# Moving the end of one norm and joining two small products in a fused attention and feed-forward kernel

## The chip, the core and the metric

The kernel runs on one core of a Trainium2 chip. The metric is the device time of one execution in microseconds (us). The core has five engines with a queue each: TensorE (PE) multiplies matrices, VectorE (DVE) and ScalarE (ACT) work elementwise, GpSimd (POOL) copies a little here, and SyncE (SP) issues most DMAs. An instruction starts when the ones ahead of it in its engine's queue have started and the semaphores that it waits for have been raised.

## The reference

An attention without softmax, normalised, is followed by a multiplicative feed-forward block, all in fp32. The batch is 8, with 8 heads, 576 tokens and 64 columns per head; the feed-forward block has 4608 tokens of width 512 and an inner width of 1024.

```python
kv = np.einsum('bhsd,bhse->bhde', k, v)
out = np.einsum('bhsd,bhde->bhse', q, kv)
rms = np.sqrt(np.mean(out * out, axis=-1, keepdims=True) + 1e-06)
attn = out / rms * g_norm
x = attn.transpose(0, 2, 1, 3).reshape(B * S, H * D)
a = x @ w1
b = x @ w2
h = a * b @ w3
result = h @ w_out
```

## The kernel before

**Algebra.** w3 and w_out are multiplied ahead of the loop into one matrix (w3o), and g_norm is multiplied into w1 and w2. The two matrix products that remain, the gates (x times w1 and w2) and the projection (a·b times w3o), are made in Strassen-Winograd form: seven products of half-sized blocks in place of eight, with sums and differences made on DVE, and, for part of the panels of the later groups and their projection, in two levels of it.

**Groups.** The 576 tokens of a batch are 512 and 64 left over. A group `T` is the 512 tokens of batch `T`; the leftovers of all eight batches make one more group. The order is `groups = [0, ..., 6, 8, 7]`, so the seventh group is `T = 6`. While the feed-forward block of group `T` runs, the attention of batch `b = T + 1` is made in pieces between its products. The pieces are lists `fs[0..7]` and `ends[0..7]` in `steps(b)`; `between()` runs one piece at fixed places. In the first group (`T = 0`, batch 1) the pieces come two in each of the panels p = 1, 2, 3 and two in the projection; `fs[2]` and `fs[3]` are the two pieces of panel 2. In the later groups two come in the one-level panel 2, four in the two-level panels (`gates_of_two`: after the third and sixth of the seven products of each of two halves of the weights), two in panel 3. There `fs[3]` follows the sixth product of the first half, and `fs[4]` the third product of the second half.

**Attention of a batch.** `begin_kv(g)` is the k-v product of four heads (L335). `product(h)` is the q-kv product of half the heads (64 matmuls of 64x64 in the trace, L413), into two PSUM banks; `product_left()` is the same for the 64 leftovers of two batches (32 matmuls, L432), made with every odd batch. Each is followed by `norm`: for each of the two banks a square on ACT (L380) and a reduce on DVE (L381); after them one square root on ACT (L385), a reciprocal (L387) and two multiplications on DVE (L390) that write `xn` or `xn_left`. `norm` is a generator with two stops, after the reduces and after the square root, so that its parts can be given different places. For batches above 2 both squares write one buffer, `sq0`, else two. The normalised `xn` is turned by a DMA: copies that split the words (L294 on ACT or POOL), a DMA transpose on SP (L298), and copies that join them (L308). q is turned in the same way (L296, L298, L308).

**Winograd panel.** `winograd` makes the seven products of a panel (L724) in PSUM banks r1, r2, r3. The copies of sums that are used again leave PSUM on ACT (L742) under the names p1, p5, u2 and u3; u3 is the sum in r1 ahead of the last product, which goes on in r1 and so waits for u3's copy. p1's copy, in these panels to `inner_sums`, frees r1 for the third product of the panel. `done` adds and multiplies on DVE (L897, L898, L894). With `copy_first` (panel 3 of the later groups) the first sum is copied from bank to bank (L751). The two-level products are L1016; their sums leave PSUM by `copy_seven` on ACT (L1065, L1066) and `add_seven` on DVE (L1069, L1070), and are finished on DVE (L1078 to L1102).

**PSUM.** There are two pools of banks, `mm` with five and `at` with three. The next bank of a pool is the one used longest ago, and its first matmul waits until the last reader is done.

**Order.** The orders of PE, POOL and SP are the program's own (`manual_schedule`). ACT and DVE, outside some stretches, are ordered at build time by a list scheduler; `tc.issue_after(x)` gives what follows a place behind the instruction `x` in that order. `slots` holds calls to be made right after a named copy, as in

```python
slots.setdefault(("p1", "p1"), []).insert(0, (all_of, rest))
```

which ends a norm behind the copy p1 in panel 1. In the first group `a.finish(0)` or `begin_first` makes the first q-kv product of the next batch; for batch 1 it is `a.finish(0)`, the whole norm at once, in the first piece of panel 2.

Of the kernel before, what the change touches and what calls it, by code (L numbers as in the profile page):

```python
# [22 lines left out]
def kernel(  # L23
# [36 lines left out]
    B, H, S, D = q.shape  # L60
# [4 lines left out]
    FIRST_OF_TWO = 2  # L65
# [12 lines left out]
    ps_at = ctx.enter_context(tc.tile_pool(name="ps_at", bufs=3, space=PSUM))  # L78
# [5 lines left out]
    def bank(pool, tag):  # L84
        return pool.tile([P, 512], FP32, name=tag, tag=tag)

    loaded, copies, adds = {}, {}, {}
# [26 lines left out]
    NF = KF // 2  # L114
# [139 lines left out]
    def all_of(steps):  # L254
        for _ in steps:
            pass
# [61 lines left out]
    def attention(b):  # L318
# [80 lines left out]
        def product(h):  # L399

            of_mm = b and (h == 0 or b <= FIRST_OF_TWO or b % 2 == 0)
            o_ps = [bank(*((ps_mm, "mm") if of_mm else (ps_at, "at"))), bank(ps_at, "at")]
            for m in range(4):
                r, e = 2 * h + m // 2, m % 2
                for i in range(2):
                    n = 2 * m + i
                    for t in range(2):
                        tokens = slice(t * L, (t + 1) * L)  # L410
                        for l in range(2):
                            rows = slice(l * D, (l + 1) * D)
                            nc.tensor.matmul(  # L413
                                o_ps[l][tokens, n * D:(n + 1) * D],
                                lhsT=qT[r][rows, e, i, tokens],
                                rhs=kv_b[rows, m // 2 ^ l, e, h, :],
                                start=True,
                                stop=True,
                            )
            xn = st[h] = work.tile([P, 2, 2, 4, D], FP32, name="xn", bufs=1)  # L420
            return norm(o_ps, [xn[:, :, l].rearrange("p i m d -> p m i d") for l in range(2)])
# [82 lines left out]
        def finish(h):  # L504
            all_of(product(h))
# [8 lines left out]
    def batch(b):  # L514
        if b not in batches:
            batches[b] = attention(b)
        return batches[b]

    slots, stage = {}, [None]

    def run_slot(key, behind):
        for f, *args in slots.pop(key, []):
            with tc.issue_after(behind.ins):
                f(*args)
# [51 lines left out]
    def steps(b):  # L576

        a = batch(b)
        a.start()
        more = b + 1 < B
        fs, ends = ([[] for _ in range(8)] for _ in range(2))

        def turn(i, f, *args, next_group=False):

            t = []

            def begin():  # L590
                t.append(f(*args))
                next(t[0])
                next(t[0])

            fs[i].append((begin,))
            (to_end if next_group else ends[i + 1]).append((lambda: all_of(t[0]),))

        if to_end:

            ends[0] += [(lambda: nc.gpsimd.tensor_copy(tick, late["p5"][:, 0, 0:1]),), *to_end]  # L600
        to_end.clear()
        odd = b % 2
        by_scalar, in_two = b >= FIRST_OF_TWO, b > FIRST_OF_TWO
        if b == 1:
            early.extend(a.q_two_by_dma(r) for r in (0, 1))
            q_first = list(early)
            fs[0].append((a.begin_kv, 0))

            def end_first():
                for t in q_first:  # L610
                    with tc.issue_after(copies["u3"][-1].ins):
                        next(t)
                    all_of(t)

            ends[1].append((end_first,))
        def begin_first():
            rest = a.product(0)
            next(rest)
            slots.setdefault(("p1", "p1"), []).insert(0, (all_of, rest))

        fs[2 if b == 1 else 1] += [
            (a.begin_kv, 1), (begin_first,) if by_scalar and not in_two else (a.finish, 0),
        ]
        if b == 1:
            last = {}

            def begin(name, behind, f, *args):
                last[name] = f(*args)
                with tc.issue_after(copies[behind][-1].ins):
                    next(last[name])  # L630
                next(last[name])

            def end(name, behind):
                with tc.issue_after(copies[behind][-1].ins):
                    next(last[name], None)
                all_of(last[name])

            fs[2].append((begin, "q2", "u2", a.q_two_by_dma, 2))
            fs[3].append((begin, "q3", "u3", a.q_two_by_dma, 3))
            fs[3].append((begin, "left", "u3", a.q_left_by_dma))  # L640
            fs[4].append((begin, "x", "u3", a.x_by_dma, 0, nc.scalar.copy))
            ends[4] += [(end, "q2", "p1"), (end, "q3", "p5")]
            ends[5] += [(end, "x", "u2"), (end, "left", "u3")]
        elif by_scalar:
            turns_by_scalar(b)
        else:
            turn(1, a.q_two_by_dma, 2, 3)
            turn(2, a.x_by_dma, 0)
            if odd:
                turn(1, a.q_left_by_dma)  # L650
        second = 5 if b == 1 else 4
        if more:
            if not (in_two and odd):
                fs[second].append((batch(b + 1).begin_kv, 0))
        fs[second].append((a.finish, 1))
        if odd:
            fs[3 if in_two else second + 1].append((a.product_left,))
        if b == 1:
            turn(6, a.x_by_dma, 1)
            turn(7, a.x_left_by_dma, next_group=True)  # L660
        else:
            if not by_scalar:
                turn(5, a.x_by_dma, 1)
            if odd:
                turn(5, a.x_left_by_dma, next_group=more)
        if more and not by_scalar:
            turn(7 if b == 1 else 5, batch(b + 1).q_two_by_dma, 0, 1, next_group=True)
        if more:
            fs[7 if odd else 0].append((load_q_left, b + 1))
        return iter([lambda s=e + f: [f(*args) for f, *args in s] for e, f in zip(ends, fs)])  # L670
# [211 lines left out]
    def gates(T, p, between, ready=lambda name: None):  # L882
        def done(name, one, two):
            multiply(name, one, two)
            ready(name)

        def multiply(name, one, two):

            dst = ab[int(name[1]) - 1][:, p, int(name[2]) - 1, :]
            if two is None:  # L890
                c = late_pool.tile([P, N], FP32, name="c21")
                copied = nc.scalar.copy(c, one[:, 0, :])
                run_slot((stage[0], name), copied)
                adds.setdefault(name, []).append(nc.vector.tensor_mul(dst, c, one[:, 1, :]))  # L894
                return
            c = late_pool.tile([P, 2, N], FP32, name="c")
            adds.setdefault(name, []).append(nc.vector.tensor_add(c, one, two))  # L897
            nc.vector.tensor_mul(dst, c[:, 0, :], c[:, 1, :])  # L898

        winograd(  # L900
            lambda name, w, c: wa[p][name][:, w, c, :],
            lambda name, c: xb[T][name][:, c, :],
            NP // 2, done, between, T == 0 or p + 1 < NF,
            places=(2, 1, 0) if T not in IN_TWO else (0, 1, 2) if p + 1 == NF else (2, 0, 1),
            copy_first=T in IN_TWO and p + 1 == NF,
            first=bank(ps_at, "at") if T in IN_TWO and p + 1 == NF and T % 2 and T + 2 < B else None,
        )


# [471 lines left out]
    IN_TWO = (*range(FIRST_OF_TWO, B - 1), *TWICE)  # L1381
# [9 lines left out]
    with tc.manual_schedule(  # L1391
# [44 lines left out]
        first = batch(0)  # L1436
# [52 lines left out]
    for n, T in enumerate(groups):  # L1489
# [29 lines left out]
        if T in IN_TWO:  # L1519
            p = 2  # L1520
            stage[0] = "p2"
            with tc.issue_after(adds["out"].ins):
                sum_x(T)
            gates(T, p, between)
            if T in TWICE:
                in_order = tc.manual_schedule(engines={mybir.EngineType.DVE})
                in_order.__enter__()
            gates_of_two(T, between)
            of_two = sum_ab_two()
            for _ in range(3):  # L1530
                of_two.pop(0)()
        else:
            of_two = []
        for p in range(NF):
# [3 lines left out]
            if T and p + 1 == NF:  # L1538
# [15 lines left out]
                gates(T, p, between, lambda name: all_of(f() for f in following[name]))  # L1554
                continue
            gates(T, p, between if T or p else lambda: None)
            if T == 0:

# [92 lines left out]
```

## Time and profile before

| | us |
|---|---|
| median of three runs | 744.86 |
| lowest and highest | 744.60, 745.33 |
| the profiled execution's own time | 745.0 |
| its span on the core | 743.1 |
| PE busy | 736.6 |
| DVE busy | 629.4 |
| ACT busy | 378.7 |

The profile is of one execution. Its own time is 1.9 us above its span; that part lies outside the recorded instructions. The granted clock of TensorE was 1.00 throughout. A row of a timeline gives the start, the duration from the first start to the last end, engine, line, operation, the output and input tiles by name, shapes, and the number of instructions; in brackets is the idle time of the engine ahead of it, and what ended that. Starts of neighbouring rows on one engine may be closer than the durations, since instructions overlap at their ends: the distance of two starts is what an instruction takes of its engine's time. The first group's panels start at 83.2 us and its last panel at 123.6 us; the seventh group runs from 531 to 603 us.

### The profile page before, as it was taken

What the parts mean: (1) busy time and instruction counts of PE and PEld (TensorE: products, weight loads), DVE (VectorE), ACT (ScalarE), POOL (GpSimd) and SP (SyncE); (2) the same over time, 40 slices, a digit from 0 to 9 for tenths busy, and PEclk for the clock granted to TensorE, in tenths of its full rate; (3) what the DMA queues carried; (4) which work ended last, traced back from release to release, by engine and by line L of the source; (5) the groups of instructions that cost most, each with busy time, mean ns of one, the idle gap of its engine ahead of it and who ended that gap; (6) DMA issues with size and microseconds to landing.
All of it is one profiled execution on the core that took longest, in us unless ns stands there. A gap on an engine that the chain in (4) does not pass through costs nothing.

```text
span 743.1 us, 16816 instructions
## 1 busy us (share of the span) xinstructions
PE 736.6 (99%) x6843; PEld 659.5 (89%) x6843; DVE 629.4 (85%) x1233; ACT 378.7 (51%) x652; POOL 21.8 (3%) x29
## 2 busy tenths in 40 slices
PE   8999999999999999999999999999999999999998
PEld 6455788888899999999999999999999999999997
DVE  6987998967869689978996899689969987997797
ACT  6687778424552575257526752576277313212321
POOL 0000000132000000010000001000001000000000
PEclk9999999999999999999999999999999999999999
DMA  9996934599999698869886988588848662565454
GB/s 307 366 321 208 263 108 122 122 331 307 281 307 321 176 264 271 267 159 284 258 265 158 304 255 263 184 279 241 278 101 220 220 212 87 176 215 162 135 198 135
DMA packets 135456, 169.65 MB, mean 228 GB/s; under 512 B 78036, under 2 KB 110804, under 8 KB 135380
## 3 DMA queue, kind: packets, MB, share of 16 engines
q1 hardware_dynamic: 132928, 154.16, 69.6%
q10 hardware_dynamic: 2452, 14.42, 5.7%
q8 instruction: 54, 0.88, 0.5%
q14 instruction: 22, 0.18, 0.1%
HBM read 130.55 MB, written 20.71 MB: 204 GB/s over the span
## 4 chain that ended last, share of the span: by engine, by line
PE 96%; DVE 1%; ACT 1%; DMA 1%; issue 0%; SPq 0%; ACTq 0%
PE mm L724 37%; PE mm L1274 23%; PE mm L1016 21%; PE mm L694 7%; PE at L335 2%; PE at L724 2%; PE at L413 1%; PE mm L413 1%; PE at L681 1%; DMA raw<-in_moe_w_out_dram 1%; PE at L1317 0%; DVE ab L162 0%; PE at L432 0%; ACT w_sb L133 0%; DVE chunks L169 0%
## 5 line engine op out<-in xcount | busy, mean ns | idle before, releaser
L1065 ACT COPY slots<-mm 128x512 f32<-128x512 f32 x88 | 51.7, 587 | 125.7 <-PE mm L1274 83.1
L724 PE MATMUL mm<-xT,w_sb 128*128 128x256 f32 x448 | 102.9, 379 | 0.0
L724 PEld LDWEIGHTS mm<-xT,w_sb 128*128 128x128 f32 x448 | 84.4, 190 | 11.5 <-issue 0.5
L724 PE MATMUL mm<-xc,ws 128*128 128x256 f32 x336 | 76.1, 379 | 0.0
L724 PEld LDWEIGHTS mm<-xc,ws 128*128 128x128 f32 x336 | 63.8, 190 | 8.7
L742 ACT COPY slots<-mm 128x512 f32<-128x512 f32 x59 | 34.6, 587 | 70.9 <-PE mm L724 65.5
L694 PE MATMUL mm<-chunks,ab 128*128 128x512 f32 x128 | 60.7, 605 | 0.7 <-DVE chunks L172 0.7
L1069 DVE TENSOR_TENSOR slots<-mm,slots 128x512 f32<-128x512 f32 x66 | 45.1, 683 | 17.3 <-PE mm L1016 17.3
L1066 ACT COPY slots<-mm 128x384 f32<-128x384 f32 x88 | 42.4, 482 | 25.8 <-PE mm L1274 23.1
L1016 PE MATMUL mm<-ws,w3o_sb 128*128 128x128 f32 x350 | 53.9, 275 | 0.0
L381 DVE TENSOR_REDUCE inv<-sq 128x8 f32<-128x512 f32 (+1 forms) x40 | 24.6, 629 | 29.9 <-ACT sq L380 29.9
L1274 PE MATMUL mm<-w3o_sb,ab 128*128 128x128 f32 x368 | 49.0, 276 | 0.0
L1016 PEld LDWEIGHTS mm<-ws,w3o_sb 128*128 128x128 f32 x350 | 46.4, 192 | 0.0
L1274 PEld LDWEIGHTS mm<-w3o_sb,ab 128*128 128x128 f32 x368 | 45.4, 192 | 0.6
L1274 PE MATMUL mm<-w3o_sb,raw 128*128 128x128 f32 x340 | 43.5, 275 | 0.0
L694 PEld LDWEIGHTS mm<-chunks,ab 128*128 128x128 f32 x128 | 21.6, 190 | 22.4 <-issue 14.4
L1274 PEld LDWEIGHTS mm<-w3o_sb,raw 128*128 128x128 f32 x340 | 40.7, 192 | 0.0
L724 PE MATMUL mm<-xc,w_sb 128*128 128x256 f32 x160 | 38.6, 384 | 0.3 <-ACT slots L742 0.3
L724 PE MATMUL mm<-xT,ws 128*128 128x256 f32 x160 | 38.1, 381 | 0.0
L1070 DVE TENSOR_TENSOR slots<-mm,slots 128x384 f32<-128x384 f32 x66 | 36.4, 551 | 1.9 <-PE mm L1274 1.9
L308 ACT COPY xT<-xn 128x1024 uint16<-128x1024 uint16 x28 | 32.5, 1168 | 3.3 <-DMA xn<-xT 3.3
L724 PEld LDWEIGHTS mm<-xc,w_sb 128*128 128x128 f32 x160 | 29.7, 190 | 4.9 <-ACT slots L742 0.7
(243 smaller groups left out, 1650.8 us busy)
## 6 DMA issues: line engine op xcount, KB each, us to landing
w3o_sb<-w_l SPq DMA_DIRECT2D x21, 896.0 KB, 4.9
w3o_sb<-w3o_l SPq DMA_DIRECT2D x18, 896.0 KB, 6.8
raw<-in_moe_w_dram SPq DMA_DIRECT2D x31, 512.0 KB, 7.4
raw<-w3o_l SPq DMA_DIRECT2D x15, 896.0 KB, 4.9
w3o_sb<-w3o_l ACTq DMA_DIRECT2D x14, 896.0 KB, 4.6
k_sb<-in_k_dram SPq DMA_DIRECT2D x16, 576.0 KB, 5.1
v_sb<-in_v_dram SPq DMA_DIRECT2D x16, 576.0 KB, 6.3
q_sb<-in_q_dram SPq DMA_DIRECT2D x32, 256.0 KB, 4.3
```

The lines of the kernel that those rows point to most:

```text
L308: copy(words(dst), src)
L335: nc.tensor.matmul(ps[r * D:(r + 1) * D, :], lhsT=k_sb[rows, r, cols], rhs=v_sb[rows, r, cols], start=(j == 0), stop=(j == JS - 1),)
L381: adds["norm"] = nc.vector.tensor_reduce(out=inv[:, i], in_=sq.rearrange("p (h d) -> p h d", d=D), axis=AX.X, op=ALU.add)
L694: nc.tensor.matmul(sums_ps[half][m], lhsT=w3T[half, c][:, m, :], rhs=chunks[:, c, 1, :], start=(c == 0), stop=(c == KF - 1),)
L724: nc.tensor.matmul(ps[:, u, :], lhsT=lhsT(a_name, u, c), rhs=rhs(b_name, c),  start=(u == 0 and c == 0 and new), stop=(c == chunks - 1), s ...
L742: copies.setdefault(name, []).append(nc.scalar.copy(t, ps))
L1016: nc.tensor.matmul(ps[place // 4][:, place % 4, :], lhsT=x, rhs=y, start=new and place // 4 not in seen, stop=True, skip_group_check=True,)
L1065: nc.scalar.copy(z[:, 0:4], ps[0])
L1066: return nc.scalar.copy(z[:, 4:7], ps[1][:, 0:3])
L1069: nc.vector.tensor_add(z[:, 0:4], ps[0], z[:, 0:4])
L1070: nc.vector.tensor_add(z[:, 4:7], ps[1][:, 0:3], z[:, 4:7])
L1274: nc.tensor.matmul(ps[place // 4][:, place % 4, :], lhsT=x[:, c, :], rhs=y[:, c, :], start=new and place // 4 not in seen, stop=(c == 1), ...
```

## The change

In the first group, the end of the first norm of batch 1 (the square root, the reciprocal, the multiplications) is no longer made in one go with its beginning. `begin_first` makes the product, the squares and the reduces; a new function `end_first_norm` in the next piece gives the square root and what follows a place behind u3's copy of panel 2. For the other batches `begin_first` does what it did.

In the seventh group, `product_left` of batch 7 moves from `fs[3]` to the front of `fs[4]`, so that its matmuls come right ahead of those of the second q-kv product, with no product of the feed-forward block between them. The first bank of that q-kv product becomes a `mm` bank in place of an `at` bank, and the first bank of panel 3 an `at` bank in place of a `mm` bank. The DMAs and copies that turn the leftovers stay in their pieces.

```diff
-            of_mm = b and (h == 0 or b <= FIRST_OF_TWO or b % 2 == 0)
+            of_mm = b and (h == 0 or b <= FIRST_OF_TWO or b % 2 == 0 or b == B - 1)
...
+        rest_of_norm = []
+
         def begin_first():
-            rest = a.product(0)
-            next(rest)
-            slots.setdefault(("p1", "p1"), []).insert(0, (all_of, rest))
+            rest_of_norm.append(a.product(0))
+            next(rest_of_norm[0])
+            if b > 1:
+                slots.setdefault(("p1", "p1"), []).insert(0, (all_of, rest_of_norm[0]))
+
+        def end_first_norm():
+            with tc.issue_after(copies["u3"][-1].ins):
+                next(rest_of_norm[0])
+            all_of(rest_of_norm[0])
 
         fs[2 if b == 1 else 1] += [
-            (a.begin_kv, 1), (begin_first,) if by_scalar and not in_two else (a.finish, 0),
+            (a.begin_kv, 1), (a.finish, 0) if in_two else (begin_first,),
         ]
+        if b == 1:
+            fs[3].append((end_first_norm,))
...
         if odd:
-            fs[3 if in_two else second + 1].append((a.product_left,))
+            at = 4 if b == B - 1 else 3 if in_two else second + 1
+            fs[at].insert(0, (a.product_left,))
...
-            first=bank(ps_at, "at") if T in IN_TWO and p + 1 == NF and T % 2 and T + 2 < B else None,
+            first=bank(ps_at, "at") if T in (*range(FIRST_OF_TWO + 1, B - 2, 2), B - 2) and p + 1 == NF else None,
```

## The prediction

> **What bounds the kernel now.** I read the page first, then the waits of TensorE (PE), then a table of windows over the panels of the first group, then the timelines of PE, ScalarE (ACT) and VectorE (DVE) around the two places that the diff touches, and last the order in which the built program issues its instructions on each engine, before and after the change. That order is fixed at build time, so the steps below can be worked out on it with durations from the trace. The page:
>
> ```profile
> PE 736.6 (99%) x6843; PEld 659.5 (89%) x6843; DVE 629.4 (85%) x1233; ACT 378.7 (51%) x652; POOL 21.8 (3%) x29
> ```
>
> PE is the bound in every stage, so a microsecond that PE waits is a microsecond of the span, and one that DVE or ACT works longer is nothing until PE waits for it. In PE's list of waits one line lies behind the start-up:
>
> ```profile
> PE mm L724 <- ACT slots L742: 0.3, 1, 0.3
> ```
>
> That is the wait which the first edit is aimed at. Its price is seen better in the windows of two panels of the first group with the same PE work (28 Winograd matmuls, one k-v product, one q-kv product):
>
> ```profile
> 108.62:123.61 14.99, 14.70 (x194) 12.55 (x193) 12.35 (x25) 11.71 (x22) 0.00 (x0) 1.00 0.45 129
> 123.61:138.03 14.42, 14.42 (x193) 12.63 (x192) 14.42 (x38) 9.58 (x13) 0.00 (x0) 1.00 0.68 135
> ```
>
> The columns are the window, its length, then busy time and count of PE, PEld, DVE, ACT, POOL, and the granted clock. The panel with the wait is 14.99 − 14.42 = 0.57 us longer, at a clock of 1.00 in both. So at most 0.57 us are to be had here.
>
> **First edit: the end of the norm behind u3's copy.** PE's timeline, ACT's and DVE's:
>
> ```profile
> 117.87 3.62 PE L724 MATMUL mm<-xT,w_sb 128*128 128x256 f32 x16
> 121.78 1.99 PE L724 MATMUL mm<-xc,w_sb 128*128 128x256 f32 x8 [0.29 <-ACT slots L742]
> 123.61 1.89 PE L724 MATMUL mm<-xT,w_sb 128*128 128x256 f32 x8
> 125.33 3.62 PE L724 MATMUL mm<-xc,ws 128*128 128x256 f32 x16
> ```
>
> ```profile
> 119.49 0.59 ACT L380 ACTIVATE sq<-at 128x512 f32<-128x512 f32 x1
> 120.94 0.31 ACT L385 ACTIVATE inv<-inv,eps_col 128x16 f32<-128x16 f32 x1 [0.86 <-DVE inv L381]
> 121.16 0.56 ACT L742 COPY slots<-mm 128x512 f32<-128x512 f32 x1
> 123.52 1.99 ACT L294 COPY xT<-xn 128x1024 uint16<-128x1024 uint16 x2
> 126.02 0.59 ACT L742 COPY inner_sums<-mm 128x512 f32<-128x512 f32 x1 [0.24 <-DVE c L897]
> ```
>
> ```profile
> 119.63 1.28 DVE L381 TENSOR_REDUCE inv<-sq 128x8 f32<-128x512 f32 x2 [2.64 <-ACT sq L380]
> 122.48 0.68 DVE L390 TENSOR_TENSOR xn<-at,inv 128x512 f32<-128x512 f32 x1
> ```
>
> The copy of u3 (121.16) stood behind the square root (120.94), which waited 0.86 us for the reduces; the last product of the panel waited for that copy. In the new order the copy stands right behind the second square: 119.97 to 120.6, before PE wants it at 121.3. The wait goes and the last panel starts at 123.61 − 0.57 = 123.04. What is late next is the same norm. On DVE the new order puts between the reduces and the second multiplication of xn (L390) three of the four sums of the next weights, and two adds ahead of it. By the starts of neighbouring rows a 128x512 operation takes 0.60 us, a 128x256 one 0.335, the reciprocal 0.16. After the reduces (120.83): five 128x512 (the add of c12, two sums ws, the sum w_sb, the add of c22) and one 128x256 between them, then the reciprocal, another 128x256, the first multiplication and the add of c11, in all 7 × 0.60 + 2 × 0.335 + 0.16 = 5.03 us. So the second multiplication starts at 125.86 and ends at 126.54, against 123.16 now: 3.4 us later.
>
> Two ACT copies xT<-xn (L294) read that xn, 0.95 us each by their starts, and the built order leaves them where they were against the next panel: ahead of its first copy, inner_sums<-mm. So that copy, queued behind a waiting instruction, now starts at 126.57 + 2 × 0.95 = 128.46 and ends at 129.05. It frees the bank into which PE's third product of the panel accumulates. That product started at 125.33 + 1.73 = 127.06 before, would be due at 126.49 after, and now waits to about 129.07: a new wait of 2.6 us where one of 0.57 went. Net 129.07 − 127.06 = 2.0, and 0.1 for the restart (the old wait cost 0.46 us of start and 0.57 of panel): **+2.1 us**. Bounds: 1.9 if the restart costs nothing, 2.4 if the next copies (two transposes' copies of 1.06 us stand between them) also come 0.2 to 0.3 us late; by the rows they come 0.2 us early. The fourth sum ws, now behind the norm, is done by 127.8 and wanted at 130.8; SP and POOL keep their order.
>
> [...] The rows show a clock of 1.00 around the present wait of 0.3 us, and no row has a wait as long as the new one.
>
> **Second edit: the leftovers' product joined to the second q-kv product.** PE's rows around the leftovers' block of the seventh group:
>
> ```profile
> 554.48 0.39 PE L1016 MATMUL mm<-sq,raw 128*128 128x128 f32 x2
> 554.79 0.69 PE L432 MATMUL at<-kv_sb,qT_left 64*64 64x64 f32 x32
> 555.42 0.71 PE L1016 MATMUL mm<-xc,w_sb 128*128 128x128 f32 x4
> 555.97 0.39 PE L1016 MATMUL mm<-ws,w_sb 128*128 128x128 f32 x2
> ```
>
> Two L1016 rows take 0.223, so the block holds PE from 554.71 to 555.97 − 0.447 = 555.52: 0.81 us. Its 32 small matmuls at 0.0145 each (64 of L413 take 0.93) are 0.46; the other 0.35 is the change to 64x64 and back, which a joined block pays once. PE gains **0.35 us**, if nothing makes it wait.
>
> Now the norms of both products come in one stretch. For these batches all squares share one buffer (sq0), so each square waits for the reduce of the one before: four handovers ACT to DVE, two of which now stand ahead of copies that PE needs. I work in the clock of before (the first edit shifts all by 2.1). The joined block starts at 561.87 − 0.81 = 561.06; after it the products of weights 3, 4, 5, 6 start at 562.71, 564.27, 565.84 and 567.40, the panel at 568.96. The DVE sums of product 1 (3.4 us from L1069 to L1084) start at 559.5 (PE goes on from that product at 560.21 − 0.81), without the old leftovers' norm ahead, and free DVE at 562.9. Then: reduce of the first leftovers' square to 563.3, second square to 563.7, reduce to 564.15, square root to 564.5, reciprocal and two multiplications to 565.4, while ACT squares the first half of the q-kv product by 565.0; its reduce 565.4 to 566.1, second square 566.14 to 566.73, and only then the second copy of product 3 (L1066):
>
> ```profile
> 565.05 0.60 ACT L380 ACTIVATE sq<-at 128x512 f32<-128x512 f32 x1 [0.31 <-DVE inv L381]
> 565.54 0.47 ACT L1066 COPY slots<-mm 128x384 f32<-128x384 f32 x1
> 568.38 1.29 DVE L390 TENSOR_TENSOR xn<-at,inv 128x512 f32<-128x512 f32 x2 [0.25 <-ACT xT L308]
> 575.39 0.59 ACT L742 COPY slots<-mm 128x512 f32<-128x512 f32 x1
> ```
>
> That copy ends at 567.1 instead of 566.0. Product 5 wants its bank at 565.84 + 0.89 = 566.73: **wait 0.4**. The add (L1069) behind the second reduce ends at 568.04; product 6 wants its bank at 567.80: **wait 0.25**. The two copies L308 behind L1066 end at 569.44, so xn (568.38 above) starts at 569.47, 1.09 late; DVE works without a pause from there, so the u2 copy (575.39) moves to 576.48 and ends at 577.07, while PE, by then 0.3 late, wants it at 576.53: **wait 0.55**. Sum: −0.35 + 0.4 + 0.25 + 0.55 = +0.85, and DVE's rest lag of 0.2 shows at most 0.1 in the projection: **+0.9 us**. Bounds: −0.35 if all three waits stay hidden, +1.5 if each is 0.2 longer than worked out.
>
> At nothing: the q-kv product's first half in a mm bank and the panel's first product in an at bank. Groups three and five have it so, and their L413 blocks and L724 products take what these take. The at bank is free from 565.5, 3.4 us ahead of its use; if it were not, PE would wait for the difference. The leftovers' multiplication ends 4.5 us later, so POOL's copy (1.04 us) and SP's transpose move with it, and the w3o load queued behind that transpose is issued at 567.9 instead of 566.15; it lands about 4.9 us later, at 572.8, and is wanted at 581.4. The copies to x_left end near 573, wanted at 591.2.
>
> **Sum.** +2.1 + 0.9 = +3.0 us: span 743.1 to 746.1, the profiled execution's own 745.0 to 748.0; against the median of the runs shown, 744.86, it is 747.9.
>
> **Rivals.** (1) Only the second edit behaves as its words say: the waits at 566.7, 567.8 and 576.5 do not come, because the handovers from ACT to DVE and back leave more room than my rows give. Then +2.1 − 0.35 = 1.75: 746.6. Against it: three separate places must hold. (2) Faster: xn is ready early enough for the two L294 copies to be out of the way. It decides at one point: the second multiplication must end by 126.49 − 0.59 − 1.90 = 124.0 us. Then both gains are net: −0.57 − 0.35 = −0.92, and with the second edit's waits hidden 743.9. For it, today's row ends at 123.16; against it, the new order has 5.0 us of DVE work ahead and DVE is busy without a pause there. (3) As rival 2 in the first group, but the second edit's waits come: −0.57 + 0.9 = +0.3: 745.2, no change. (4) The lag spreads: the next copies of the first group's last panel come late too, and each wait of the second edit is longer: +2.4 + 1.5 = 3.9: 748.8.
>
> **How the numbers follow.** Forecast 0.72, rival 1 0.14, rival 2 0.03, rival 3 0.03, rival 4 0.08. The range takes in forecast, rival 1 and rival 4: 746.6 to 748.9. About 0.2% (1.5 us) is what a measurement of this kernel can tell from no change; faster by that 0.03, within it 0.04, slower 0.93.
>
> **What would show it.** Right: no PE wait on u3's copy; a new PE wait of about 2.6 us in the first group's last panel, released by ACT's inner_sums copy, with L294 ahead of it starting near 126.6; three short PE waits in the seventh group; the L432 and L413 rows in one stretch. Wrong: xn done by 124, an ACT copy inner_sums ahead of L294, or no PE wait behind the joined block.

## The result and the profile after

| | before | after |
|---|---|---|
| median, us | 744.96 (744.60 to 745.33, 6 runs) | 748.48 (747.68 to 750.10, 6 runs) |
| ratio | | 1.005, 95% interval 1.0037 to 1.0063 |
| profiled execution, own time and span | 745.0, 743.1 | 750.1, 748.2 |
| mean granted clock of the profiled execution | 1.000 | 0.998 |

The change makes the kernel 3.5 us slower. The prediction was 747.9 us with a range of 746.6 to 748.9. The profiled execution of after is one of the longer ones. In the changed kernel every line number from L617 on is larger by up to 11: L724 is L735, L742 is L753, L1016 is L1027, L1066 is L1077. The whole trace of after lies 0.24 us later than that of before from the start-up on, ahead of both edits; this is taken off where starts are compared.

TensorE's waits after, behind the start-up (us in total, times, longest):

```profile
PE mm L735 <- ACT inner_sums L753: 2.4, 1, 2.4
...
PE mm L1027 <- ACT slots L1077: 0.3, 1, 0.3
PE at L735 <- ACT slots L753: 0.3, 1, 0.3
```

The wait on u3's copy is gone, and a wait of 2.4 us on the inner_sums copy has come. The last two lines are of the seventh group. The first group, on PE's, ACT's and DVE's timelines of after:

```profile
121.56 1.89 PE L735 MATMUL mm<-xc,w_sb 128*128 128x256 f32 x8
123.29 1.89 PE L735 MATMUL mm<-xT,w_sb 128*128 128x256 f32 x8
125.02 1.89 PE L735 MATMUL mm<-xc,ws 128*128 128x256 f32 x8
129.29 2.98 PE L735 MATMUL mm<-xc,ws 128*128 128x256 f32 x8 [2.38 <-ACT inner_sums L753]
132.06 2.64 PE L735 MATMUL mm<-xT,ws 128*128 128x256 f32 x8
```

```profile
120.20 0.59 ACT L753 COPY slots<-mm 128x512 f32<-128x512 f32 x1
121.17 0.31 ACT L385 ACTIVATE inv<-inv,eps_col 128x16 f32<-128x16 f32 x1 [0.38 <-DVE inv L381]
...
126.77 1.99 ACT L294 COPY xT<-xn 128x1024 uint16<-128x1024 uint16 x2 [2.85 <-DVE xn L390]
128.66 0.58 ACT L753 COPY inner_sums<-mm 128x512 f32<-128x512 f32 x1
```

```profile
126.05 0.68 DVE L390 TENSOR_TENSOR xn<-at,inv 128x512 f32<-128x512 f32 x1
```

u3's copy (120.20) stands ahead of the square root (121.17), and its product (121.56) no longer waits. The second multiplication of xn starts at 126.05, the two L294 copies wait for it, and the inner_sums copy stands behind them, at 128.66. PE's third product of the panel waits for it until 129.29.

One thing in these rows was not expected: the two products behind the wait take 2.77 and 2.48 us by their starts, and a product of this form takes 1.73 to 1.84. The windows of after over the wait and these two products (length, then busy time and count of PE, PEld, DVE, ACT, POOL, then the granted clock), and the same of a run with the first edit alone:

```profile
126.75:129.29 2.54, 0.16 (x1) 0.00 (x0) 2.54 (x8) 2.52 (x4) 0.00 (x0) 1.00 0.00 0
129.29:132.06 2.77, 2.77 (x8) 2.25 (x9) 2.77 (x10) 2.56 (x3) 0.00 (x0) 0.66 0.11 38
132.06:134.54 2.48, 2.48 (x10) 2.08 (x9) 1.30 (x4) 0.58 (x1) 0.00 (x0) 0.70 0.76 218
```

```profile
126.75:129.29 2.54, 0.15 (x1) 0.00 (x0) 2.54 (x8) 2.52 (x4) 0.00 (x0) 1.00 0.00 0
129.29:131.13 1.84, 1.83 (x9) 1.63 (x10) 1.84 (x7) 1.84 (x3) 0.00 (x0) 1.00 0.00 0
131.13:132.85 1.72, 1.72 (x9) 1.52 (x8) 1.72 (x6) 1.22 (x2) 0.00 (x0) 1.00 0.47 152
```

The idle stretch is the same in both, 2.54 us long with PE busy for the first 0.15. In after the clock then falls to half; by the trace's records of the clock for 3.41 us, from 130.16 on, 0.87 us after PE had gone on. This costs (2.77 − 1.84) + (2.48 − 1.72) = 1.69 us. In the other execution it stays at 1.00.

The seventh group, PE and ACT:

```profile
565.00 0.69 PE L432 MATMUL at<-kv_sb,qT_left 64*64 64x64 f32 x32
...
571.19 0.49 PE L1027 MATMUL mm<-ws,raw 128*128 128x128 f32 x2 [0.34 <-ACT slots L1077]
...
581.14 1.99 PE L735 MATMUL at<-xT,w_sb 128*128 128x256 f32 x8 [0.26 <-ACT slots L753]
```

```profile
567.18 0.38 ACT L380 ACTIVATE sq<-at 128x256 f32<-128x256 f32 x1 [1.05 <-DVE inv L381]
...
570.17 0.60 ACT L380 ACTIVATE sq<-at 128x512 f32<-128x512 f32 x1 [0.86 <-DVE inv L381]
570.67 0.47 ACT L1077 COPY slots<-mm 128x384 f32<-128x384 f32 x1
```

The second square of each norm waits for a reduce, and the copy L1077, which PE waits for at 571.19, stands behind the last of them.

The profiled execution adds up. Against before PE is 0.24 us late at the start, 4.02 in the second group (so first edit 2.10 and clock 1.68 between) and 5.11 in the projection of the seventh group (second edit 1.09).

### The profile page after: what moved, and what is told of

It reads as the page before. It is cut to its first block, busy times and chain, and to the rows that moved or that the text cites. A ratio compares the mean times of both kernels' runs of the same rounds, so it can differ in the third digit from the quotient of the medians.

```text
span 748.2 us, 16823 instructions
## 1 busy us (share of the span) xinstructions
PE 739.1 (99%) x6843; PEld 661.3 (88%) x6843; DVE 629.8 (84%) x1233; ACT 378.7 (51%) x652; POOL 21.4 (3%) x29
## 3 DMA queue, kind: packets, MB, share of 16 engines
q10 hardware_dynamic: 2452, 14.42, 5.7%
## 4 chain that ended last, share of the span: by engine, by line
PE 92%; DVE 4%; ACT 2%; issue 1%; DMA 1%; SPq 0%; ACTq 0%; DVEq 0%
PE mm L735 35%; PE mm L1285 23%; PE mm L1027 19%; PE mm L705 7%; PE at L335 2%; PE at L735 2%; PE mm L413 1%; PE at L413 1%; PE at L692 1%; DMA raw<-in_moe_w_out_dram 1%; PE at L1328 0%; DVE inv L381 0%; DVE ab L162 0%; ACT w_sb L133 0%; ACT xT L308 0%
## 5 line engine op out<-in xcount | busy, mean ns | idle before, releaser
L735 PE MATMUL mm<-xT,w_sb 128*128 128x256 f32 x432 | 99.3, 379 | 0.0
L735 PEld LDWEIGHTS mm<-xT,w_sb 128*128 128x128 f32 x432 | 81.5, 190 | 11.0 <-issue 0.5
L735 PE MATMUL mm<-xc,ws 128*128 128x256 f32 x328 | 75.6, 383 | 2.4 <-ACT inner_sums L753 2.4
L735 PEld LDWEIGHTS mm<-xc,ws 128*128 128x128 f32 x328 | 62.8, 192 | 11.3 <-ACT inner_sums L753 2.8
L753 ACT COPY slots<-mm 128x512 f32<-128x512 f32 x58 | 34.0, 586 | 74.0 <-PE mm L735 68.0
L1077 ACT COPY slots<-mm 128x384 f32<-128x384 f32 x88 | 42.3, 481 | 26.1 <-PE mm L1285 23.4
L1027 PE MATMUL mm<-ws,w3o_sb 128*128 128x128 f32 x350 | 54.0, 275 | 0.0
L1027 PEld LDWEIGHTS mm<-ws,w3o_sb 128*128 128x128 f32 x350 | 46.4, 192 | 0.0
L735 PE MATMUL mm<-xT,ws 128*128 128x256 f32 x160 | 38.9, 387 | 0.0
L735 PE MATMUL mm<-xc,w_sb 128*128 128x256 f32 x152 | 36.6, 384 | 0.0
L735 PEld LDWEIGHTS mm<-xT,ws 128*128 128x128 f32 x160 | 30.9, 195 | 4.4
L308 ACT COPY xT<-xn 128x1024 uint16<-128x1024 uint16 x28 | 32.5, 1168 | 0.9 <-DMA xn<-xT 0.9
```

Of the source, the lines that this page charges most:

```text
L308: copy(words(dst), src)
L735: nc.tensor.matmul(ps[:, u, :], lhsT=lhsT(a_name, u, c), rhs=rhs(b_name, c),  start=(u == 0 and c == 0 and new), stop=(c == chunks - 1), s ...
L753: copies.setdefault(name, []).append(nc.scalar.copy(t, ps))
L1027: nc.tensor.matmul(ps[place // 4][:, place % 4, :], lhsT=x, rhs=y, start=new and place // 4 not in seen, stop=True, skip_group_check=True,)
L1077: return nc.scalar.copy(z[:, 4:7], ps[1][:, 0:3])
```

## The experiments

Times are medians, with before at 744.98 us (first four runs) or 745.07 (the others). "Net" is the shift of PE's starts in the run's own trace, with the shift of its start-up taken off.

**The first edit alone.** The three lines of the second edit are put back.

> The first edit alone (the second undone). Theory A (ScalarE's two L294 copies of xn, queued ahead of the last panel's inner_sums copy, hold TensorE): one TensorE wait of about 2.4 us released by that copy at 126.8 us, and +2.1 us against before (about 747.0) in executions whose clock stays at 1.00; where a period of 3.4 us at half clock follows the wait, 1.7 us more (about 748.7). Theory B (the first edit carries the whole measured +3.5 and the second costs nothing): a median near 748.5 with the clock at 1.00. In both the seventh group's waits are those of before.

747.18, 747.26, 748.76, 748.77 and 748.93 us. The two short ones have a mean clock of 1.000, the three long ones of 0.998. The profiled one (747.26) has the wait of 2.4 us and a net of +2.10. So theory A holds with both its heaps, 1.6 us apart, and theory B falls: the median of 748.76 is near its number, but not at a clock of 1.00, and the second edit has its own price:

**The second edit alone.**

> The second edit alone. Theory A (the two norms in one stretch share one square buffer, and the copies that TensorE needs queue behind the squares): waits of about 0.3, 0.25 and 0.3 us in the seventh group and +0.9 to +1.1 us: 745.8 to 746.1, with no spread, the clock at 1.00, since each wait is short. Rival (the handovers stay hidden and only the saved change of matmul size counts): -0.35, 744.6.

746.09 us (745.83 to 746.62, 11 runs), ratio 1.0012 (1.0004 to 1.0021), net +1.07, the clock at 1.00. PE's starts tell the terms, set against its shift just ahead of the seventh group: the joined block brings −0.35; the fifth product starts 0.15 late (a wait of 0.51), the sixth 0.43 (0.28 more), the product behind u2's copy 0.96 (0.53), the projection 1.14 (0.18). Each delay but the first includes the slower restart behind the one before it, 0.10 us (the product that has waited, at 577.15, takes 1.83 us by its start, the one ahead of it, at 573.27, 1.73). With these, the three waits cost 0.61, 0.28 and 0.53.

**The first edit with L294 behind u2's copy.**

```diff
-            fs[4].append((begin, "x", "u3", a.x_by_dma, 0, nc.scalar.copy))
+            fs[4].append((begin, "x", "u2", a.x_by_dma, 0, nc.scalar.copy))
```

> The first edit alone, and the two L294 copies given a place behind the last panel's u2 copy, so that the inner_sums copy and the next two stand ahead of them. Theory A (the order on ScalarE is the cause): no TensorE wait in the first group's last panel, neither the old one of 0.3 on u3's copy, clock 1.00, and -0.3 to -0.57 us: 744.3 to 744.6. Rival (the late end of the norm on VectorE is itself the cause: the inner_sums copy must wait for the c11 addition that still reads inner_sums, and that is late too): a wait of 0.5 to 1 us stays in front of the third product, 745.0 or more.

744.64 us (744.28 to 745.04, 11 runs), ratio 0.9994 (0.9985 to 1.0003), net −0.32. Neither wait is in PE's list; the order on ScalarE was the cause. The rival names something real that is just hidden. ACT, then PE, of this run:

```profile
126.03 0.58 ACT L752 COPY inner_sums<-mm 128x512 f32<-128x512 f32 x1 [2.33 <-DVE c L907]
```

```profile
124.80 3.86 PE L734 MATMUL mm<-xc,ws 128*128 128x256 f32 x16
```

The copy does wait for the c11 addition, and ends at 126.61, when PE wants the bank at 126.53; the pair of products takes 3.86 us where 3.62 is usual. So of the 0.56 us that the edit frees 0.24 is lost there. The gain over the kernel before, 0.34 us by the medians, lies within the interval and was not measured a second time.

**The wait filled with matmuls.** This is the first edit alone with matmuls ahead of the waiting product, and with the L308 copies of x given a place behind u3's copy:

```diff
+            if name == "p5" and len(copies[name]) == NF:
+                warm = bank(ps_at, "at")
+                for _ in range(20):
+                    nc.tensor.matmul(warm[:, 0:P], lhsT=ident, rhs=ident, start=True, stop=True)
...
-            ends[5] += [(end, "x", "u2"), (end, "left", "u3")]
+            ends[5] += [(end, "left", "u3"), (end, "x", "u3")]
```

> The first edit alone, with 20 additional 128x128 matmuls (about 0.11 us each, 2.2 us) into an unused bank right ahead of the waiting product, and the L308 copies of x placed behind u3's copy, where they stand without that. TensorE still waits as long in sum, but is idle for only about 0.3 us of it. Theory A with the clock (the idle stretch is what lets the clock fall): the same +2.1 us as the plain wait, 747.0, the clock at 1.00 in the profile and no execution near 748.7. Rival (the longer executions have another cause than the idle stretch): the spread of 747 to 749 stays.

748.96 us (748.65 to 749.23, 5 runs): my filling was twice too long. PE's row lists 40 instructions for these 20 fp32 matmuls, two for each; they took 4.47 us (126.73 to 131.20) and held PE beyond the copy. The time says nothing of the wait's price; but there is one heap only, and the clock is 1.00. With 10:

> As the run with the filled wait, but with 10 additional matmuls, each of which is two instructions of 0.112 us: 2.23 us, so that they end before the inner_sums copy does and TensorE is idle for 0.3 us in place of 2.4. If the idle stretch lets the clock fall: +2.0 to +2.2 us in every execution, 747.0 to 747.2, the clock at 1.00, no execution near 748.8. Rival (the clock falls for another reason than the idle stretch): two heaps, 747.2 and 748.8, as with the first edit alone.

747.09 us (746.85 to 748.05, 10 runs), every mean clock 0.999 or 1.000; nine of ten lie within 0.7 us. PE's rows:

```profile
126.25 2.39 PE L757 MATMUL at<-ident 128*128 128x128 f32 x20
128.81 1.99 PE L734 MATMUL mm<-xc,ws 128*128 128x256 f32 x8 [0.17 <-ACT inner_sums L752]
```

The product waits as long as before and costs the same 2.1 us, but PE is idle for 0.17 us of it, and the upper heap is gone. So in these runs the fall of the clock goes with the idle stretch, 2.4 us against 0.17, and not with the lateness.

**Half the wait.** One of the two L294 copies goes to POOL:

```diff
+            return together([x_part_by_dma(0, 0, nc.scalar.copy), x_part_by_dma(0, 1, nc.gpsimd.tensor_copy)])
...
-            fs[4].append((begin, "x", "u3", a.x_by_dma, 0, nc.scalar.copy))
+            fs[4].append((begin, "x", "u3", a.x_by_two))
```

> The first edit alone, but only one of the two L294 copies of x on ScalarE (0.95 us of its queue); the other, and the L308 copy that belongs to it, on POOL. If what TensorE waits for is ScalarE's queue, the wait on the inner_sums copy is shorter by one copy: 2.4 - 0.95 = 1.45 us, and the time +1.0 to +1.1 us: 746.1. The clock: an idle stretch of 1.6 us instead of 2.5; if a shorter stretch doesn't let the clock fall, one heap at 746.1 with the clock at 1.00; if it does, a second heap near 747.8.

746.51 us (746.23 to 747.67, 11 runs), 0.4 above the expected 746.1, though the net, +1.16, is as expected; of its 11 mean clocks none is below 0.999. PE:

```profile
128.33 1.99 PE L737 MATMUL mm<-xc,ws 128*128 128x256 f32 x8 [1.45 <-ACT inner_sums L755]
```

The wait is shorter by just the copy that left the queue, and no second heap comes.

**The changed kernel again.**

> The changed kernel once more, for the spread of its executions. With the first edit at +2.0, the second at +1.05 and 1.7 us more in the executions in which the clock falls after the long wait, the times should come in two heaps, near 748.1 (clock 1.00) and near 749.8 (mean clock 0.998). Rival (the spread has several causes and no heaps): times strewn evenly from 747.6 to 750.1.

749.89 us (749.32 to 750.12, 5 runs). With the six runs of the result, six executions have a mean clock of 0.997 or 0.998, and these lie at 749.6 to 750.1. That heap is as expected. The other five are no heap: 747.68, 747.69, 748.34, 748.62 and 749.32 around the expected 748.1. What strews them is not settled.

**The leftovers' squares in a buffer of their own** (second edit alone).

```diff
+                if b == B - 1 and w < G:
+                    sq = st["qT"].rearrange("p r t -> p (r t)")[:, i * w:(i + 1) * w]
```

> The second edit alone, but the squares of the leftovers' norm go to a buffer of their own (qT_left, which nothing reads after its product), so that they don't wait for the reduces of the buffer sq0. If the handovers on the shared buffer make the first two waits (0.46 and 0.28 us in the run of the second edit), those go and the third, before u2's copy, stays: -0.34 + 0.5 + 0.1 = +0.3 us, 745.3. Rival (the waits come of the later place of the work on VectorE as such): all three stay, +1.05, 746.0.

745.88 us (745.41 to 746.84, 11 runs), net +0.53. The first wait (0.61 with its restart) is gone; the second (0.28) and the third (0.53) stay. The theory holds for the leftovers' pair of squares, which is all that this edit frees; the q-kv product's two still share sq0. So both pairs were freed:

**No square waits for a reduce** (second edit alone): the leftovers' squares in the halves of sq0, the q-kv product's first in qT_left.

```diff
+                if b == B - 1 and w == G and i == 0 and "left" in st:
+                    sq = st["qT"].rearrange("p r t -> p (r t)")
+                else:
+                    part = i * w if b == B - 1 and w < G else 0
```

> The second edit alone, with the squares so placed that none waits for the reduce of the one before: both squares of the leftovers in two halves of sq0, the first square of the second q-kv product in qT_left, the second in sq0. If the shared buffer makes the waits: the second L1067-like copy of product 3 goes back to about 566 us, xn is 0.8 to 1 us earlier than with the second edit, the first two waits go and the third (0.53 us, before u2's copy) shrinks to 0.3 or less: -0.34 + 0.3 = 0, 744.8 to 745.2. Rival (VectorE has too much to do in that stretch in any order): the third wait stays at 0.5, 745.3 or more.

745.79 us (745.14 to 748.12, 12 runs), net +0.72. The first two waits shrink from 0.89 to 0.10 in sum, restarts included, and xn starts at 568.75 in place of 569.50, as expected, but the third wait grows to 0.91. DVE and POOL show a part of why:

```profile
570.54 0.43 DVE L1102 TENSOR_TENSOR slots<-slots 128x256 f32<-128x256 f32 x1
570.88 0.75 DVE L1085 TENSOR_TENSOR slots<-slots 128x128 f32<-128x128 f32 x1
```

```profile
569.97 1.52 POOL L308 COPY x_left<-xn_left 128x512 uint16<-128x512 uint16 x2 [3.14 <-DMA xn_left<-qT_left]
```

The small addition (0.28 us with the second edit) takes 0.75, from 570.88 to 571.63; POOL's copies, 569.97 to 571.49, take 1.52 in place of 1.28. Each is longer where the two overlap. So u2's copy starts only 0.28 us earlier than with the second edit (576.23 against 576.51), while PE arrives 0.66 earlier. Without the 0.47 us that DVE lost, my estimate of the third wait is still about 0.45, above the expected 0.3: DVE's work in that stretch stays a cause beside POOL's copies.

**Both edits mended**: L294 behind u2, the leftovers' squares in qT_left, and the end of the leftovers' norm in the next piece, behind the q-kv product's squares and reduces.

```diff
+            if b < B - 1:
+                all_of(rest)
+            st["rest"] = rest
...
+                fs[5].append((lambda: all_of(a.rest_left()),))
```

> Both edits, mended: L294 behind the last panel's u2 copy, the leftovers' squares in qT_left, and the end of the leftovers' norm (square root, reciprocal, multiplications) one piece later, behind the beginning of the second q-kv product's norm. If the causes are the ones named: the first edit gives -0.46 and the second -0.34 with at most 0.2 us of waits left: 744.2 to 744.5, the clock at 1.00. Rival (the norm's late end in the seventh group delays the panel's u2 copy in any order): 744.8 or more.

746.31 us (745.63 to 746.71, 11 runs): missed by 1.8 us. In the trace the first edit gives −0.32, +0.73 comes at 182 to 188 us, and the seventh group costs +1.04. There the same addition, longer still, beside a copy on POOL:

```profile
570.68 1.15 DVE L1100 TENSOR_TENSOR slots<-slots 128x128 f32<-128x128 f32 x1
```

```profile
570.64 1.04 POOL L296 COPY qT_left<-xn_left 128x1024 uint16<-128x1024 uint16 x1 [105.48 <-DVE xn_left L393]
```

So I took that copy away from POOL:

```diff
+        def apart_by_scalar(to, src):
+            return (first_copy.pop() if first_copy else nc.gpsimd.tensor_copy)(to, src)
...
-                turn(5, a.x_left_by_dma, next_group=more)
+                turn(5, a.x_left_by_dma, *([apart_by_scalar] if b == B - 1 else []), next_group=more)
```

> As the run with both edits mended, but the copy of xn_left (L296) that ran on POOL from 570.64 to 571.68, while one VectorE addition of 128x128 took 1.15 us in place of 0.28, is made by ScalarE; the two copies at the end of that turn stay on POOL. If POOL's copy held VectorE up: that addition takes 0.3 us again, u2's copy comes 0.85 us earlier, and of the two waits in the seventh group (0.8 and 0.4 us) at most 0.2 is left: 1 us less than the mended run, 745.1 to 745.4, or 744.6 where the wait of 0.5 us at 182 us doesn't come either. Rival (that addition was slow for another reason): it stays at 1.15 us and the time at 746.3.

745.27 us (744.32 to 746.95, 12 runs), ratio 1.0002 (0.9994 to 1.0011). DVE again:

```profile
570.52 0.28 DVE L1105 TENSOR_TENSOR slots<-slots 128x128 f32<-128x128 f32 x1
```

The addition is back at 0.28 us, the wait at u2's copy is gone, and the seventh group costs a net of +0.19: POOL's copy was the cause. What remains in this trace is +0.41 at 182 to 188 us. The orders on DVE and ACT up to there are those of the run with L294 behind u2; what differs is when the transpose of x lands, and so when ACT's L308 copies, ahead of the next norm's squares, can start: 135.96 before, 136.51 in the run with L294 behind u2, 136.79 and 136.98 in the last two. With 136.51 the lag on DVE is covered, with the others it is not. This is read from the traces and was not tried, and it does not explain why the latest of them costs less (0.41) than the one before (0.73).

No version is clearly faster than the kernel before. The nearest is the first edit with L294 behind u2's copy, without the second edit: 0.34 us less, within the uncertainty.

## Why the prediction held, and where it did not

- **The old wait goes.** Foretold: the last panel 0.57 us earlier (123.04). Measured: 0.56 (123.05), with the start's shift taken off, and a panel of 14.42 us. Right.
- **The new wait.** Foretold: second multiplication at 125.86, L294 near 126.6, third product at 129.07, +2.1. Measured, less the 0.24: 125.81, 126.53, 129.05, +2.10 in the run of the first edit alone. Right, and shown to be the queue order by the runs with L294 elsewhere. The lower bound of 1.9 is a slip: without the restart the sum is 2.0.
- **The clock.** Here a step failed: the sum has no term for it, and no run had shown what so long a wait does to the clock; that it adds nothing was my assumption. In after PE was idle for 2.38 us and the clock fell to half for 3.41 us, which cost 1.69. By the mean clocks (0.997 or 0.998) it fell in 9 of the 16 executions with that wait (6 of 11 with both edits, 3 of 5 with the first alone), in none of the 11 with 1.45 us and none of the 10 with 0.17. The 1.7 us stood in no case and no chance: the range ends at 748.9, and the six executions of the changed kernel with the fall lie at 749.6 to 750.1. That the median of 748.48 is in the range is luck: only two of its six executions were of that kind. Over all eleven of the changed kernel the median is 749.60, above the range.
- **The second edit.** Foretold −0.35, +0.4, +0.25, +0.55, up to +0.1, in sum +0.9. Measured −0.35, +0.51, +0.28, +0.53, +0.18, in sum +1.14 within the group (+1.07 over the whole trace). Right in mechanism and place; the first wait is short by 0.1, and so is what follows the third, where the restarts of 0.10 that were counted for the first edit were left out.
- **Its cause.** Right for the first two waits: without shared squares 0.89 us of them, restarts included, becomes 0.10. The third was foretold as DVE's lag behind xn; it went only when the leftovers' norm was out of the way and POOL's copy with it. Which share each of these two has was not measured apart.
- **At nothing.** The banks, POOL's copy and the w3o load cost nothing in after, as foretold. That POOL's copy could cost something, where it meets other work on DVE, was not seen; two experiments ran into it.
- **Rivals.** Rival 1 (the second edit's waits stay hidden) and rivals 2 and 3 (xn ready by 124.0; it ends at 126.5 with the start's shift taken off) are out. Rival 4's time, 748.8, is near the median, but its mechanism, longer waits, is not what happened.

## What to carry to other kernels

When the end of a chain is moved on a shared engine, list what its consumers stand ahead of in their own queues: here two copies that wait for xn held a copy that TensorE needed, and another place for the two copies was worth 2.4 us. Price a wait of the bounding engine twice, by its length and by what the clock does behind it: here 2.1 us, and 1.69 more in the trace of after. A step that is moved takes its helpers along to new neighbours; a copy of 1.04 us on POOL cost 0.87 us of DVE's time (an addition of 1.15 in place of 0.28) where it landed beside that addition.

## What the runs showed of the hardware

In the trace of after the clock is recorded at 1.00 from 7.28 us to 130.16, at half for 3.41 us, and at 1.00 again until 747.97. PE had been idle for 2.38 us and had resumed 0.87 us before that fall, which cost 1.69 us. By the mean clocks the same happened in 9 of the 16 executions with this wait. Its length alone does not tell which: the profiled run of the first edit alone has the same stretch of 2.54 us with PE busy for 0.15, and a clock of 1.00 in the windows behind it (129.29 to 132.85), where the changed kernel again, idle for 2.40 us, has 0.64 (129.29 to 134.00). With a wait of 1.45 us the profiled clock stayed at 1.00 (127 to 136 us), with one of 0.17 too (127 to 136 us). What sets the nine executions apart from the other seven was not shown.

A DVE addition of 128x128 with both inputs in SBUF took 1.15 us beside POOL's L296 copy (both edits mended), 0.75 beside its L308 copies (no square waits for a reduce), and 0.28 with that L296 copy on ACT. In the first of these POOL's copy ran from 570.64 to 571.68 and the addition from 570.68 to 571.83. In before, POOL's copy at 561.26 (1.04 us) runs beside two additions that have one input in PSUM (L1069 at 560.96, 0.68 us; L1070 at 561.55, 0.55), and the same two lines take 0.68 and 0.55 at 566.28 and 569.59, where no copy runs on POOL. What makes an addition longer beside a copy was not shown.
